# Layer 2's second products in seven instead of eight for six of eight feature groups, with paired wide operations

## The chip, the core and the metric

One NeuronCore of a Trainium2 chip runs the whole program. The metric is device time in microseconds, from the program's start to its end; the times shown are the median of several executions. The engines are TensorE (PE; its weight loads have a row of their own, PEld), VectorE (DVE), ScalarE (ACT), GpSimd (POOL) and SyncE (SP), which issues most of the DMA transfers.

## What is computed

Attention over 256 channels and two feed-forward layers, all in float32, on 6016 tokens:

```python
qn = q / (norm(q, axis=1) + 1e-06); kn = k / (norm(k, axis=1) + 1e-06)
s = kn.transpose(0, 2, 1) @ qn / tau          # 256 x 256
a = exp(s - s.max(-1)); a /= a.sum(-1) + 1e-09
x = (v @ a).reshape(6016, 256)
h = x @ w_in                                  # 256 -> 2048
x = (h * clip(h + 3, 0, 6) / 6) @ w_out       # layer 1, 2048 -> 256
h = maximum(x @ w_in2, 0)                     # 256 -> 2048
out = (h * h) @ w_out2                        # layer 2, 2048 -> 256
```

## The kernel before

**Precision.** A float32 operand is split into a high part (a copy to a 32-bit matmul format, on ACT) and a low part (the operand less its high part, on DVE). One product of a 128x128 weight block and n columns is three matmuls: high by high, low by high, high by low.

**Tiling.** The tokens go in six *pairs* of two column blocks of n columns: n is 512 in five pairs and 448 in the last. The 2048 features go in eight *groups* of 256, two row blocks of 128. So a group's first products form a 2x2 by 2x2 block product, and so do its second products. The main loop walks over layer, pair and group; each iteration records its operations.

**Seven products for eight.** A 2x2 block product takes eight products, or seven in Strassen's manner (Winograd's variant) with sums of operands beforehand and sums of results behind. First products are done in seven almost everywhere; the sums of the tokens' blocks are t1 to t4, made in `tokens`. Second products of layer 2 are done in seven for the groups in `S2SET`: of pairs 1 to 4 the groups 0, 2, 4, 6, of pair 5 the groups 0, 2, 4. Their operands are three of the squared blocks themselves (`items_direct`: d2, d3, d1) and four sums t1 to t4 (`items_sums`: t5 takes t1, t7 takes t3, t6 takes t2, t4 takes t4). The other groups do eight (`items_plain`).

**A group of layer 2 from pair 1 on** (`first7s`). Seven first products p1, p2, p6, p7, p5, p4, p3 go into two PSUM banks X and Y by turns. ACT copies X or Y out (`snap`, L1589), DVE adds the next result (`total`, L1595) into one of four result blocks R0 to R3, and ReLU and square follow: on ACT (L1602, L1608) for three of them, on DVE (L1615) for one. A bank is taken again by the next product, which therefore waits for that copy or that sum. Then each block is split (`split`, L1623 on ACT, L1627 on DVE). For a group by seven, `tail` makes t1 by a DVE sum (L1680) and t3, t2, t4 by three transfers that POOL issues and that add a block to another in SBUF (`move`, L1637), each waiting for the one before. The second products of a group run among the first products of the next; its four sums run one group later still:

```python
t, d = us.get(k - 3), us[k - 1]
t7, t6, t4, t5 = items_sums(t) if t and t["seven"] else [None] * 4
...
gaps = [[t7], [], [d2], [], [d3], [d1], [t6, t5, t4]]
```

`gaps[i]` are the second products that stand behind the i-th first product on PE.

**Tokens.** While a pair runs, the next pair's tokens come from DRAM in four parts, one per group (L758); DVE makes t3 first (L780), which needs the last part. All seven operands are split (ACT L803, DVE L806) into a ring of `XS` = 9 tiles. The sums t1 to t3 have a three-block tile.

**What sets the order.** Every operation is recorded with an engine, a cost, a latency and what it depends on. PE and SP keep the order of recording. For DVE, ACT and POOL the planner (`Plan.issue`) plays the program once with these costs and takes among the ready operations the one with the earliest due time (`late`), so each engine gets one fixed order. At run time each engine takes its instructions in that order and waits at the first that is not ready.

Of the kernel before, what the change touches and what calls it, by code (L numbers as in the profile page):

```python
# [27 lines left out]
class Plan:  # L28
# [8 lines left out]
    URGENT = 6.0  # L37

# [14 lines left out]
    @staticmethod  # L53
    def pick(t, ready):

        for o in sorted(ready, key=lambda o: (max(t, o.can), o.late, o.n)):
            start = max(t, o.can)
            if not any(
                x.late < o.late - Plan.URGENT and start < x.can < start + o.cost for x in ready
            ):  # L60
                return start, min(
                    (x for x in ready if x.can <= start), key=lambda x: (x.late, x.n)
                )
        raise AssertionError

    def issue(self):
        def flat(d):
            if isinstance(d, Op):
                return [d]
            return [x for y in d or () for x in flat(y)]  # L70

        ops = self.ops
        for o in ops:
            o.deps = flat(o.deps)
        users = {id(o): [] for o in ops}
        now = 0.0
        for o in ops:
            for d in o.deps:
                users[id(d)].append(o)
            o.late = float("inf")  # L80
            if o.eng == "PE":
                o.late = now
                now += o.cost
        queue = float("inf")
        for o in reversed(ops):
            for u in users[id(o)]:
                o.late = min(o.late, u.late - o.lat - o.cost)
            if o.eng == "DMA":

                o.late = queue = min(o.late, queue - o.cost)  # L90
# [4 lines left out]
        for n, o in enumerate(ops):  # L95
            o.n, o.left, o.can = n, len(o.deps), 0.0
            if o.eng in in_order:
                in_order[o.eng].append(o)
            elif not o.left:
                ready[o.eng].append(o)  # L100
        order = []
        while len(order) < len(ops):
# [15 lines left out]
            o.start = start  # L118
# [11 lines left out]
        for o in order:  # L130
            o.fn()
# [6 lines left out]
def dve_us(n):  # L138
    return 0.07 + 0.00104 * n
# [24 lines left out]
def tile_kernel(  # L164
# [50 lines left out]
    XS, GB, WB = 9, 4, 2  # L215
# [530 lines left out]
    def tokens(l, pr, parts=False):  # L746
# [28 lines left out]
        def tt(i):  # L775
            return t["t"][:, i, :n]

        def f_t3():
            t["t"] = xr_p.tile([P, 3, TB], F32, tag="t", name=f"xt{l}{pr}")
            V.tensor_tensor(tt(2), b(1, 1), b(0, 1), ALU.subtract)  # L780

        if plain(l, pr):
            todo = [(f"b{i + 1}{j + 1}", lambda i=i, j=j: b(i, j), load) for j in range(2) for i in range(2)]
            ts = []
        else:
            c = dve_us(n)
            sub = ALU.subtract
            t3 = ordered("xt", add("DVE", c, f_t3, load, xt_r.take()))
            t1 = add("DVE", c, lambda: V.tensor_tensor(tt(0), b(0, 1), b(0, 0), sub), t3)
            t2 = add("DVE", c, lambda: V.tensor_tensor(tt(1), b(1, 1), tt(0), sub), t1)  # L790
            t4 = add("DVE", c, lambda: V.tensor_tensor(b(0, 1), b(1, 0), tt(1), sub), t2)
            ts = [t1, t2, t3, t4]
            todo = [
                ("b11", lambda: b(0, 0), load), ("b21", lambda: b(1, 0), load), ("t3", lambda: tt(2), t3),
                ("t2", lambda: tt(1), t2), ("t4", lambda: b(0, 1), t4), ("t1", lambda: tt(0), t1),
                ("b22", lambda: b(1, 1), load),
            ]
        for name, src, ready in todo:
            p = {}

            def f_hi(p=p, name=name, src=src):
# [3 lines left out]
            def f_lo(p=p, src=src):  # L805
# [5 lines left out]
            if ts:  # L811
                xt_r.reader(hi, lo)
            x_op[l, pr, name], x_done[l, pr, name], x_held[l, pr, name] = p, (hi, lo), x_r.last
        xr_r.reader(*ts)
# [619 lines left out]
    S2SET = {pr: (0, 2, 4, 6) if pr < NP - 1 else (0, 2, 4) for pr in range(1, NP)}  # L1434
    S2ALL = sorted({g for gs in S2SET.values() for g in gs})

# [3 lines left out]
    class Cell:  # L1440
        def __init__(self, make, deps=()):
            self.make, self.held, self.at = make, list(deps), None
# [70 lines left out]
    def extra_cells():  # L1513
# [3 lines left out]
        deps = all_of(stage_r)  # L1517
        for k in range(2, 4):
            cells["x", k] = Cell(lambda: stage_p.tile([P, 2, 4, P], F32R, tag="stage", name="w2x"), deps)
        cells["st"] = Cell(lambda: stage_p.tile([P, 2, 512], F32, tag="stage", name="rs"), deps)  # L1520

    def more_cells():
        deps = all_of(cv_r)
# [4 lines left out]
        st = cells["st"]  # L1528
        s0, s1 = (Cell(part_of(st, k), st.held) for k in range(2))
        deps = all_of(rt_r)  # L1530
        rt = [Cell(lambda: pools["r"].tile([P, 2, TB], F32, tag="r", name="rp"), deps) for _ in range(2)]
        rp = [Cell(part_of(x, k), deps) for x in rt for k in range(2)]
        cells["R", True] = [[e[0], e[1], m[0], m[1]], [e[2], m[2], s0, s1]]
        cells["R", False] = [rp]
        deps = all_of(wA_r)
        g4 = [Cell(lambda: wA.tile([P, 2, TB], F32R, tag="wA", name="gs"), deps) for _ in range(4)]
        deps = all_of(g_r)
        for _ in range(4):
            x = Cell(lambda: pools["g"].tile([P, 2, 2, TB], F32R, tag="g", name="gs"))
            g4.extend(Cell(part_of(x, k), deps) for k in range(2))  # L1540
        names = ["d3", "d2", "d1", "t1", "t3", "t2", "t4", "p0", "p2", "p3", "p1", "d0"]
        cells.update(zip(names, g4))
        deps = all_of(h_r)
        cells["f5"] = [Cell(lambda: h_p.tile([P, TB], F32, tag="h", name="f5"), deps) for _ in range(2)]
        deps = all_of(hp_r)
        hp = [Cell(lambda: pools["hp"].tile([P, 2, TB], F32, tag="hp", name="hs")) for _ in range(2)]
        q = [Cell(part_of(x, k), deps) for x in hp for k in range(2)]
        cells["fz"], cells["s1"] = q[:2], q[2]
        cells["X"], cells["Y"] = (Cell(lambda: psum("A", "xy"), [A_r.take()]) for _ in range(2))

    def bank_cells(k):
# [3 lines left out]
        )[4 * k - 4 : 4 * k]:  # L1555
            cells[name] = Cell(lambda tag=tag: psum(tag, tag), all_of(ring))

    def first7s(pr, g):
# [4 lines left out]
        even = g % 2 == 0  # L1563
        sets = cells["R", even]
        R = sets[g // 2 % len(sets)]
        names = ("d0", "d1", "d2", "d3") if even else ("p0", "p1", "p2", "p3")
# [32 lines left out]
        def relu(k, src, *deps):  # L1599
            return add(  # L1600
                "ACT", act_us(n) + 0.08,
                lambda: A.activation(R[k].ap()[:, :n], src.ap()[:, :n], AF.Relu), *deps,  # L1602
            )

        def square(k, *deps):
            def f():
                r = R[k].ap()[:, :n]
                A.activation(r, r, AF.Square)  # L1608

            return add("ACT", act_us(n), f, *deps)  # L1610

# [7 lines left out]
        def split(k, cell, *deps):  # L1619
            c = cells[cell]  # L1620

            def f_hi():
                A.activation(c.ap()[:, 0, :n], R[k].ap()[:, :n], AF.Copy)  # L1623
# [434 lines left out]
```

## Time and profile before

| | |
|---|---|
| median of 3 runs | 1030.91 us (1029.73 to 1032.05) |
| the profiled execution | 1029.68 us, its span 1027.9 us |
| PE busy | 1020.8 us, 99% of the span, 4565 matmuls recorded |
| PE weight loads | 854.9 us, 83% |
| DVE, ACT busy | 866.5 us (84%), 795.3 us (77%) |
| POOL busy | 69.4 us (7%) |
| DMA | 174.10 MB; hardware queue 45.3%, software queue 8.3% of 16 engines' span |

Attention takes the first 50 us or so, layer 1 and the first pair of layer 2 run to about 626 us, and pairs 1 to 5 of layer 2 fill the rest; a pair takes about 79 us and a group a little under 10. Busy time of an engine is the union of its instructions' times. Matmuls overlap at their ends, so two matmuls that start 0.34 us apart still show as busy all the time between them; the starts tell more than the busy share.

### The profile page before, as it was taken

What the parts mean: (1) busy time and instruction counts of PE and PEld (TensorE: products, weight loads), DVE (VectorE), ACT (ScalarE), POOL (GpSimd) and SP (SyncE); (2) the same over time, 40 slices, a digit from 0 to 9 for tenths busy, and PEclk for the clock granted to TensorE, in tenths of its full rate; (3) what the DMA queues carried; (4) which work ended last, traced back from release to release, by engine and by line L of the source; (5) the groups of instructions that cost most, each with busy time, mean ns of one, the idle gap of its engine ahead of it and who ended that gap; (6) DMA issues with size and microseconds to landing.
All of it is one profiled execution on the core that took longest, in us unless ns stands there. A gap on an engine that the chain in (4) does not pass through costs nothing.

```text
span 1027.9 us, 13018 instructions
## 1 busy us (share of the span) xinstructions
PE 1020.8 (99%) x4565; PEld 854.9 (83%) x4565; DVE 866.5 (84%) x1372; ACT 795.3 (77%) x1287; POOL 69.4 (7%) x78
## 2 busy tenths in 40 slices
PE   9999999999999999999999999999999999999998
PEld 8888888888888888888998888788888878888897
DVE  4999988888989898898878977689888878888876
ACT  6787667677777777677768878889889879789785
POOL 3400000000000000000000000111111111111110
PEclk9999999999999999999999999999999999999999
DMA  9658347344544544635744424755665565565661
GB/s 363 262 178 249 125 152 230 135 146 177 172 161 160 193 169 150 230 106 197 266 152 171 149 72 135 204 134 141 180 162 149 156 176 133 169 176 123 169 160 45
DMA packets 62609, 174.10 MB, mean 169 GB/s; under 512 B 6992, under 2 KB 10192, under 8 KB 61264
## 3 DMA queue, kind: packets, MB, share of 16 engines
q1 hardware_dynamic: 54336, 158.62, 45.3%
q0 software_dynamic: 8208, 14.65, 8.3%
q8 instruction: 36, 0.59, 0.2%
q14 instruction: 29, 0.24, 0.1%
HBM read 126.35 MB, written 32.24 MB: 154 GB/s over the span
## 4 chain that ended last, share of the span: by engine, by line
PE 95%; DVE 2%; ACT 1%; DMA 1%; issue 0%; SPq 0%; DVEq 0%
PE acc L1361 10%; PE acc L1362 10%; PE acc L1367 10%; PE xy L1577 6%; PE xy L1579 6%; PE xy L1578 6%; PE A L1268 4%; PE A L1269 4%; PE A L1270 4%; PE s L900 4%; PE acc L1713 3%; PE acc L1715 3%; PE acc L1714 3%; PE B L1268 2%; PE B L1270 2%; PE B L1269 2%
## 5 line engine op out<-in xcount | busy, mean ns | idle before, releaser
L1362 PE MATMUL acc<-g,wo 128*128 128x512 f32 (+1 forms) x448 | 173.0, 386 | 0.0
L1361 PE MATMUL acc<-g,wo 128*128 128x512 f32 (+1 forms) x448 | 173.0, 386 | 0.0
L1154 DVE TENSOR_TENSOR g<-r,g 128x1024 fp32r<-128x1024 f32 (+1 forms) x112 | 135.0, 1205 | 24.0 <-ACT g L1150 23.8
L1150 ACT ACTIVATE g<-r 128x1024 fp32r<-128x1024 f32 (+1 forms) x112 | 117.1, 1046 | 46.4 <-DVE r L1124 45.7
L1367 PE MATMUL acc<-g,wo 128*128 128x512 f32 (+1 forms) x448 | 136.5, 386 | 0.0
L1637 POOL DMA_DIRECT2D rs<-rs x57 | 49.2, 862 | 915.8 <-ACT rp L1589 607.5
L1627 DVE TENSOR_TENSOR gs<-rs,gs 128x512 fp32r<-128x512 f32 (+1 forms) x137 | 90.0, 673 | 18.3 <-ACT gs L1623 16.7
L1367 PEld LDWEIGHTS acc<-g,wo 128*128 128x128 f32 x448 | 84.2, 188 | 16.0
L1361 PEld LDWEIGHTS acc<-g,wo 128*128 128x128 f32 x448 | 84.2, 188 | 15.9
L1362 PEld LDWEIGHTS acc<-g,wo 128*128 128x128 f32 x448 | 84.1, 188 | 15.9
L1623 ACT ACTIVATE gs<-rs 128x512 fp32r<-128x512 f32 (+1 forms) x137 | 80.1, 614 | 7.9 <-DVE rs L1615 7.6
L1119 ACT ACTIVATE r<-hp,three 128x1024 f32<-128x1024 f32 (+1 forms) x40 | 45.3, 1131 | 48.9 <-DVE hp L1301 48.8
L1293 ACT ACTIVATE hp<-A 128x512 f32<-128x512 f32 (+1 forms) x96 | 56.5, 589 | 9.2 <-PE A L1270 8.2
L1577 PE MATMUL xy<-xt,w 128*128 128x512 f32 (+1 forms) x160 | 63.1, 395 | 0.1
L1579 PE MATMUL xy<-xt,w 128*128 128x512 f32 (+1 forms) x160 | 61.7, 386 | 0.0
L1578 PE MATMUL xy<-xt,w 128*128 128x512 f32 (+1 forms) x160 | 61.7, 386 | 0.0
L1124 DVE SCALAR_TENSOR_TENSOR r<-r,hp 128x1024 f32<-128x1024 f32 (+1 forms) x40 | 47.9, 1197 | 15.8 <-ACT r L1119 15.4
L1627 DVE TENSOR_TENSOR gs<-rp,gs 128x512 fp32r<-128x512 f32 (+1 forms) x80 | 52.3, 670 | 5.6 <-ACT gs L1623 5.6
L1595 DVE TENSOR_TENSOR rp<-xy,rp 128x512 f32<-128x512 f32 (+1 forms) x60 | 40.4, 674 | 17.3 <-ACT rp L1589 14.2
L1713 PE MATMUL acc<-gs,wo 128*128 128x512 f32 (+1 forms) x141 | 54.3, 385 | 0.2 <-DVE c L1827 0.2
L1715 PE MATMUL acc<-gs,wo 128*128 128x512 f32 (+1 forms) x141 | 54.3, 385 | 0.0
L1714 PE MATMUL acc<-gs,wo 128*128 128x512 f32 (+1 forms) x141 | 54.3, 385 | 0.0
(376 smaller groups left out, 2617.3 us busy)
## 6 DMA issues: line engine op xcount, KB each, us to landing
w<-w1d SPq DMA_DIRECT2D x176, 448.0 KB, 4.3
rs<-rs POOLq DMA_DIRECT2D x48, 256.0 KB, 3.3
qk<-in_qk_dram SPq DMA_DIRECT2D x8, 1024.0 KB, 15.0
w1d<-wA SPq DMA_DIRECT2D x16, 448.0 KB, 5.6
xr<-in_vT_dram SPq DMA_DIRECT2D x5, 1024.0 KB, 6.8
x2d<-o SPq DMA_DIRECT2D x20, 256.0 KB, 3.8
w1d<-wA SPq DMA_DIRECT2D x16, 256.0 KB, 2.6
w1d<-w SPq DMA_DIRECT2D x14, 256.0 KB, 3.0
```

What stands on the lines that cost most here:

```text
L1150: A.activation(t["g"][:, a:b, 0, :n], t["t"][:, a:b, :n], AF.Copy)
L1154: V.tensor_tensor(g[:, a:b, 1, :n], t["t"][:, a:b, :n], g[:, a:b, 0, :n].bitcast(F32), ALU.subtract)
L1361: T_.matmul(acc[b, e][:, :n], w(e, 0), gh_, start=first_of, stop=False)
L1362: T_.matmul(acc[b, e][:, :n], w(e, 1), gh_, start=False, stop=False)
L1367: T_.matmul(acc[b, e][:, :n], w(e, 0), gl_, start=False, stop=last_of_b)
L1577: T_.matmul(ps, wh, xh, start=start, stop=False, skip_group_check=True)
L1578: T_.matmul(ps, wl, xh, start=False, stop=False, skip_group_check=True)
L1579: T_.matmul(ps, wh, xl, start=False, stop=True, skip_group_check=True)
L1627: V.tensor_tensor(x[:, 1, :n], R[k].ap()[:, :n], x[:, 0, :n].bitcast(F32), ALU.subtract)
L1713: T_.matmul(ps, wh, gh, start=first, stop=False, skip_group_check=True)
L1714: T_.matmul(ps, wl, gh, start=False, stop=False, skip_group_check=True)
L1715: T_.matmul(ps, wh, gl, start=False, stop=last, skip_group_check=True)
```

## The change

Six groups of eight do their second products in seven: 0, 1, 3, 4, 5, 6 of pairs 1 to 4 and 0, 1, 3, 4, 5 of pair 5. So 29 groups instead of 19.

The result blocks now stand in two tiles of two blocks each (`Duo`): A2 holds R0 and R1, B2 holds R2 and R3. There are three such sets, on the spaces `stage`, `r` and `hp` (`RSET`); the remaining groups (2 and 7, of pair 5 groups 2 and 6) use single blocks. With a set, ReLU and square of R2 and R3, and their split, are one operation of 2n columns each; R0's ReLU and square go to DVE instead of R3's. Of the four sums, t3 and t2 are made by one transfer of twice the width that adds R2, read twice, to R0 and R1, and t4 by a second transfer; their splits are one wide and one single. The four sums' products no longer run two groups behind a group but at the places in `S2AT`, three to four groups behind; t1's product joins the direct ones.

`tokens` makes t1, t2 and t4 in place of the token blocks, so the third tile shrinks to one block and the ring of operand tiles grows to 10. Six instead of four sets of weight sums are made (`sums2`), in the first pair of layer 2.

The planner plays the program 200 times; after each time `blame` lowers the rank of the operations on which PE waited, and the order of the shortest play is kept.

```diff
+    ROUNDS = 200
...
+    def blame(self):
+        for o in self.ops:
+            if o.eng != "PE" or o.idle < 0.03:
+                continue
+            x = o
+            while x.deps:
+                x = max(x.deps, key=lambda d: d.start + d.cost + d.lat)
+                if x.eng in ("PE", "DMA") or o.start - x.start > 12.0:
+                    break
+                x.rank -= 0.5 * min(1.0, o.idle + 0.2)
...
+        for _ in range(self.ROUNDS):
+            end, order = self.run()
+            if best is None or end < best[0]:
+                best = end, order
+            self.blame()
...
-    XS, GB, WB = 9, 4, 2
+    XS, GB, WB = 10, 4, 2
...
+        t3 = ordered("xt", add("DVE", dve_us(n), f_t3, load, xt_r.take()))
+        t1 = less((0, 1), (0, 1), (0, 0), t3)
+        b11 = split_x("b11", lambda: b(0, 0), load)
+        b21 = split_x("b21", lambda: b(1, 0), load)
+        t2 = less((0, 0), (1, 1), (0, 1), t1, b11)
+        t4 = less((1, 0), (1, 0), (0, 0), t2, b21)
...
-    S2SET = {pr: (0, 2, 4, 6) if pr < NP - 1 else (0, 2, 4) for pr in range(1, NP)}
+    S2SET = {pr: (0, 1, 3, 4, 5, 6) if pr < NP - 1 else (0, 1, 3, 4, 5) for pr in range(1, NP)}
+    S2AT = {0: 4, 1: 5, 3: 6, 4: 7, 5: 9, 6: 10}
+    LAST_AT = {(NP - 1, 5): 8}
...
+        rs = [Duo(lambda: stage_p.tile([P, 2, TB], F32, tag="stage", name="rs"), deps) for _ in range(2)]
...
+            h, lo = ((x[:, :, k, :n] if size > 1 else x[:, k, :n]) for k in range(2))
+            V.tensor_tensor(lo, src.ap()[..., :n], h.bitcast(F32), ALU.subtract)
...
-                nc.gpsimd.dma_start(R[k].ap()[:, :n], R[j].ap()[:, :n], accum_op=ALU.add)
+                s = src.ap()[:, :n]
+                if size > 1:
+                    s = s.unsqueeze(1).to_broadcast([P, size, n])
+                nc.gpsimd.dma_start(dst.ap()[..., :n], s, accum_op=ALU.add)
...
+            if B2:
+                r = act(AF.Relu, 0.08, B2, B2, 2, h22, h21)
+                done[2] = done[3] = act(AF.Square, 0, B2, B2, 2, r)
...
+        def chain():
...
+            x = split(R[1], part("t14", 0), 1, t1)
+            u["t1"] = (part("t14", 0), *x)
+            done["t32"] = move(A2, R[2], 2, x, done[2])
+            done["t4"] = move(R[3], R[1], 1, done["t32"], u[3][1:])
+        def split_t():
+            x = split(A2, cells["t32"], 2, done["t32"])
+            u["t3"], u["t2"] = (part("t32", 0), *x), (part("t32", 1), *x)
+            c = part("t14", 1)
+            u["t4"] = (c, *split(R[3], c, 1, done["t4"]))
...
-                    gaps = [[t7], [], [d2], [], [d3], [d1], [t6, t5, t4]]
+            if d and d["seven"]:
+                d["chain"]()
+                d2, d3, d1, t5 = items_direct(d)
+                for i, x in zip((4, 5, 6, 6), (d2, d3, d1, t5)):
+                    gaps[i].append(x)
+            elif d:
+                x = items_plain(d)
+                for i, j in zip((0, 2, 4, 5, 6, 6, 6, 6), (0, 4, 1, 3, 6, 2, 7, 5)):
+                    gaps[i].append(x[j])
+            if t:
+                t7, t6, t4 = items_t(t)
+                gaps[0].append(t7)
+                gaps[2].append(t6)
+                gaps[6].insert(-1, t4)
...
+            us[k]["splits"]()
+            if k + 1 in due:
+                us[due[k + 1]]["split_t"]()
```

**Order on PE.** The middle of one group of pair 3 (xy: the banks X and Y; xt1 to xt3: the tokens' sums; acc01, acc11: result banks of d2 and t6). Before:

```order
L1577 MATMUL xy_5584<-xt2_6795,w1_7158 128x512
L1578 MATMUL xy_5584<-xt2_6795,w1_7158 128x512
L1579 MATMUL xy_5584<-xt2_6795,w1_7158 128x512
L1713 MATMUL acc01_5681<-gs_5640,wo14_5021 128x512
L1714 MATMUL acc01_5681<-gs_5640,wo14_5021 128x512
L1715 MATMUL acc01_5681<-gs_5640,wo14_5021 128x512
L1577 MATMUL xy_5600<-xt3_6785,w1_7158 128x512
L1578 MATMUL xy_5600<-xt3_6785,w1_7158 128x512
L1579 MATMUL xy_5600<-xt3_6785,w1_7158 128x512
L1577 MATMUL xy_5584<-xt1_6833,w1_7158 128x512
L1578 MATMUL xy_5584<-xt1_6833,w1_7158 128x512
L1579 MATMUL xy_5584<-xt1_6833,w1_7158 128x512
```

Now:

```order
L1620 MATMUL xy_5601<-xt2_6745,w1_7115 128x512
L1621 MATMUL xy_5601<-xt2_6745,w1_7115 128x512
L1622 MATMUL xy_5601<-xt2_6745,w1_7115 128x512
L1778 MATMUL acc11_5916<-gs_5858,w2x_5378 128x512
L1779 MATMUL acc11_5916<-gs_5858,w2x_5378 128x512
L1780 MATMUL acc11_5916<-gs_5858,w2x_5378 128x512
L1620 MATMUL xy_5614<-xt3_6766,w1_7115 128x512
L1621 MATMUL xy_5614<-xt3_6766,w1_7115 128x512
L1622 MATMUL xy_5614<-xt3_6766,w1_7115 128x512
L1620 MATMUL xy_5601<-xt1_6785,w1_7115 128x512
L1621 MATMUL xy_5601<-xt1_6785,w1_7115 128x512
L1622 MATMUL xy_5601<-xt1_6785,w1_7115 128x512
```

Between the first products on xt2 and xt3 stands now t6, of a group three to four back, and d2 of the group just before has moved behind the product on xt1.

**Order on DVE.** Pair 3, where the next pair's tokens (xr14) are first used (xt14: the tile of t3; rp, rs, hs: result blocks). Before:

```order
L1627 TENSOR_TENSOR gs_5673<-rs_5653,gs_5673 128x512
L1627 TENSOR_TENSOR gs_5768<-rs_5803,gs_5768 128x512
L1680 TENSOR_TENSOR rs_5653<-rs_5653,rs_5594 128x512
L1595 TENSOR_TENSOR rp_5668<-xy_5600,rp_5668 128x512
L780 TENSOR_TENSOR xt14_7277<-xr14_7088 128x512
L789 TENSOR_TENSOR xt14_7277<-xr14_7088 128x512
L1595 TENSOR_TENSOR rp_5686<-xy_5584,rp_5686 128x512
L1627 TENSOR_TENSOR gs_5732<-rp_5668,gs_5732 128x512
```

Now:

```order
L1638 TENSOR_TENSOR rp_5696<-xy_5614,rp_5696 128x512
L1663 TENSOR_TENSOR gs_5719<-rs_5612,gs_5719 128x512
L1645 SCALAR_TENSOR_TENSOR rp_5671<-rp_5671 128x512
L1813 TENSOR_TENSOR f5_5742<-xy_5614,f5_5742 128x512
L802 TENSOR_TENSOR xt14_7267<-xr14_6964 128x512
L812 TENSOR_TENSOR xb11_7238<-xr14_6964,xb11_7238 128x512
L1638 TENSOR_TENSOR hs_5823<-xy_5614,hs_5823 128x512
L1663 TENSOR_TENSOR gs_5679<-rp_5696,gs_5679 128x2x512
L1663 TENSOR_TENSOR gs_5719<-hs_5840,gs_5719 128x512
```

Before, t3 (L780) stood behind the first sum of group 5 (rp_5668). Now it (L802) stands behind all sums of group 5 (rp_5671, rp_5696) and its Y bank's last flush (L1813), at the first sum of group 6 (hs_5823). Both orders are alike in pairs 2 to 4.

**Order on ACT.** One group by seven (rp: its blocks; L1632 is the copy of a bank). Now:

```order
L1632 ACTIVATE rp_5671<-xy_5601 128x512
L1658 ACTIVATE gs_5698<-rs_5612 128x512
L1632 ACTIVATE rp_5696<-xy_5601 128x512
L1658 ACTIVATE gs_5858<-hs_5823 128x2x512
L1632 ACTIVATE rp_5696<-xy_5614 128x512
L1658 ACTIVATE gs_5719<-rs_5612 128x512
L1652 ACTIVATE rp_5671<-xy_5601 128x512
L1652 ACTIVATE rp_5696<-rp_5696 128x1024
L1652 ACTIVATE rp_5671<-rp_5671 128x512
L1652 ACTIVATE rp_5696<-rp_5696 128x1024
L1632 ACTIVATE rs_5746<-xy_5601 128x512
```

Before, the same stretch held single operations only. Now a wide split (gs_5858) stands ahead of the third copy, and a wide square ahead of the next group's first copy.

The built program has 4418 matmul instructions where it had 4448, all 30 fewer in layer 2. On DVE the splits' low parts and t1's sums were 217 + 19 single operations; they are 129 + 29 single and 59 wide. On ACT the ReLUs and squares from SBUF and the splits were 417 single operations; they are 209 single and 119 wide. POOL issued 57 single moves; it issues 29 single and 29 wide. Up to the first pair of layer 2 the orders differ only in the tokens' sums and in a few exchanged neighbours.

## Rows read from the trace of the kernel before

**Rows 1.** Page, part 1: busy time, share, instructions; part 2: granted clock

```profile
PE 1020.8 (99%) x4565; PEld 854.9 (83%) x4565; DVE 866.5 (84%) x1372; ACT 795.3 (77%) x1287; POOL 69.4 (7%) x78
PEclk9999999999999999999999999999999999999999
```

**Rows 2.** Stretches: us, busy (instructions) by engine, granted clock, DMA share, GB/s

```profile
300.00:400.00 100.00, 100.00 (x443) 82.86 (x442) 92.70 (x142) 76.61 (x109) 0.00 (x0) 1.00 0.45 155
578.00:617.00 39.00, 39.00 (x174) 32.31 (x173) 32.28 (x56) 30.07 (x42) 0.00 (x0) 1.00 0.24 82
697.00:776.00 79.00, 79.00 (x348) 64.88 (x347) 67.10 (x109) 67.77 (x125) 10.31 (x12) 1.00 0.60 160
776.00:855.00 79.00, 78.23 (x342) 63.50 (x341) 65.54 (x106) 66.53 (x122) 10.31 (x12) 1.00 0.59 158
855.00:934.00 79.00, 78.95 (x347) 64.44 (x346) 66.27 (x108) 67.34 (x124) 10.32 (x12) 1.00 0.58 155
```

**Rows 3.** Timeline of PE, pair 3: start us, us, instruction, [idle before <-releaser]

```profile
838.14 0.39 PE L1577 MATMUL xy<-xt,w 128*128 128x512 f32 x1
838.37 0.39 PE L1578 MATMUL xy<-xt,w 128*128 128x512 f32 x1
...
839.28 0.39 PE L1715 MATMUL acc<-gs,wo 128*128 128x512 f32 x1
840.39 0.50 PE L1577 MATMUL xy<-xb,w 128*128 128x512 f32 x1 [0.72 <-DVE rp L1595]
840.72 0.39 PE L1578 MATMUL xy<-xb,w 128*128 128x512 f32 x1
...
845.06 0.39 PE L1579 MATMUL xy<-xb,w 128*128 128x512 f32 x1
845.49 0.50 PE L1577 MATMUL xy<-xt,w 128*128 128x512 f32 x1
845.83 0.39 PE L1578 MATMUL xy<-xt,w 128*128 128x512 f32 x1
```

**Rows 4.** Timeline of PE, pair 5

```profile
1014.34 0.37 PE L1577 MATMUL xy<-xb,w 128*128 128x448 f32 x1
1014.54 0.37 PE L1578 MATMUL xy<-xb,w 128*128 128x448 f32 x1
```

**Rows 5.** Waits: engine line <- waited for: us in total, times, longest us

```profile
PEld xy L1577 <- DVE rp L1595: 4.8, 15, 1.1
```

**Rows 6.** Timelines of DVE and SP (its DMA issues), pair 3

```profile
835.24 0.68 DVE L1595 TENSOR_TENSOR rp<-xy,rp 128x512 f32<-128x512 f32 x1
838.44 0.69 DVE L780 TENSOR_TENSOR xt<-xr 128x512 f32<-128x512 f32 x1 [2.52 <-DMA xr<-x2d]
839.04 0.68 DVE L789 TENSOR_TENSOR xt<-xr 128x512 f32<-128x512 f32 x1
839.65 0.68 DVE L1595 TENSOR_TENSOR rp<-xy,rp 128x512 f32<-128x512 f32 x1
...
830.87 0.43 SPq L758 DMA_DIRECT2D xr<-x2d  x1
```

**Rows 7.** Groups of instructions, narrow and wide: busy us, mean ns of one | idle before

```profile
L1154 DVE TENSOR_TENSOR g<-r,g 128x1024 fp32r<-128x1024 f32 (+1 forms) x112 | 135.0, 1205 | 24.0 <-ACT g L1150 23.8
L1627 DVE TENSOR_TENSOR gs<-rs,gs 128x512 fp32r<-128x512 f32 (+1 forms) x137 | 90.0, 673 | 18.3 <-ACT gs L1623 16.7
L1150 ACT ACTIVATE g<-r 128x1024 fp32r<-128x1024 f32 (+1 forms) x112 | 117.1, 1046 | 46.4 <-DVE r L1124 45.7
L1623 ACT ACTIVATE gs<-rs 128x512 fp32r<-128x512 f32 (+1 forms) x137 | 80.1, 614 | 7.9 <-DVE rs L1615 7.6
L501 DVE TENSOR_TENSOR op<-op 128x128 f32<-128x128 f32 x28 | 7.0, 285 | 0.1
L1637 POOL DMA_DIRECT2D rs<-rs x57 | 49.2, 862 | 915.8 <-ACT rp L1589 607.5
```

**Rows 8.** DMA: software queue's share; issues xcount, KB each, median us to landing

```profile
q0 software_dynamic: 8208, 14.65, 8.3%
w<-w1d SPq DMA_DIRECT2D x176, 448.0 KB, 4.3
rs<-rs POOLq DMA_DIRECT2D x48, 256.0 KB, 3.3
wo<-wo2d SPq DMA_DIRECT2D x4, 512.0 KB, 5.8
DMA to landing us min/median/max: 3.4/5.3/7.5
```

More of the change, by code (lines that the diff above doesn't have):

```diff
@@ L54, in pick, with run @@
     def pick(t, ready):
-        for o in sorted(ready, key=lambda o: (max(t, o.can), o.late, o.n)):
+        for o in sorted(ready, key=lambda o: (max(t, o.can), o.rank, o.n)):
             start = max(t, o.can)
             if not any(
-                x.late < o.late - Plan.URGENT and start < x.can < start + o.cost for x in ready
+                x.rank < o.rank - Plan.URGENT and start < x.can < start + o.cost for x in ready
             ):
                 return start, min(
-                    (x for x in ready if x.can <= start), key=lambda x: (x.late, x.n)
+                    (x for x in ready if x.can <= start), key=lambda x: (x.rank, x.n)
                 )
         raise AssertionError
[L66 to L90, printed above, removed]
+    def run(self):
+        ops, users = self.ops, self.users
         in_order = {"PE": [], "DMA": []}
@@ L94, in issue @@
         at = {"PE": 0, "DMA": 0}
-        for n, o in enumerate(ops):
-            o.n, o.left, o.can = n, len(o.deps), 0.0
+        for o in ops:
+            o.left, o.can, o.idle = len(o.deps), 0.0, 0.0
             if o.eng in in_order:
@@ L117, in issue @@
             start, o = best
-            o.start = start
+            o.start, o.idle = start, start - free[o.eng]
             free[o.eng] = start + o.cost
@@ L773, in b, with split_x, f_hi, f_lo @@
             return t["r"][:, i, j * n : (j + 1) * n]
-        def tt(i):
-            return t["t"][:, i, :n]
         def f_t3():
[L779 to L798, printed above, removed]
+            t["t"] = xr_p.tile([P, TB], F32, tag="t", name=f"xt{l}{pr}")
+            V.tensor_tensor(t["t"][:, :n], b(1, 1), b(0, 1), ALU.subtract)
+        def split_x(name, src, ready):
             p = {}
-            def f_hi(p=p, name=name, src=src):
+            def f_hi():
                 p["x"] = x_p.tile([P, 2, TB], F32R, tag="x", name=f"x{name}")
                 A.activation(p["x"][:, 0, :n], src(), AF.Copy)
-            def f_lo(p=p, src=src):
+            def f_lo():
                 V.tensor_tensor(p["x"][:, 1, :n], src(), p["x"][:, 0, :n].bitcast(F32), ALU.subtract)
@@ L1562, in first7s @@
         seven = by7(l, pr, g)
[L1563 to L1566, printed above, removed]
+        A2, B2 = cells["R"][RSET[pr, g]] if (pr, g) in RSET else (None, None)
+        R = A2.part + B2.part if A2 else cells["R4"]
         X, Y = cells["X"], cells["Y"]
@@ L1650, in steps @@
             Y.use(h11)
-            g0 = square(0, relu(0, R[0], h11))
-            if not seven:
-                u[0] = split(0, names[0], g0)
+            done[0] = both(0, h11)
             yield
@@ L1662, in steps @@
             h22 = total(3, X, p5, sn7)
-            g3 = both(3, h22)
-            u[3] = split(3, names[3], g3)
+            if not B2:
+                done[3] = act(AF.Square, 0, R[3], R[3], 1, act(AF.Relu, 0.08, R[3], R[3], 1, h22))
             yield
@@ L1693, in steps, with part, splits @@
-            if seven:
-                u["tail"] = tail
-            yield
+            done[1] = act(AF.Square, 0, R[1], R[1], 1, r)
+            yield
+        def part(name, k):
+            return cells[name].part[k]
+        def splits():
+            if B2:
+                x = split(B2, cells["d23"], 2, done[2])
+                u[2], u[3] = (part("d23", 0), *x), (part("d23", 1), *x)
+            else:
+                for k in (2, 3):
+                    c = part("d23", k - 2)
+                    u[k] = (c, *split(R[k], c, 1, done[k]))
+            if seven:
+                c = cells["d1"]
+                u[1] = (c, *split(R[1], c, 1, done[1]))
+            else:
+                for k in (0, 1):
+                    c = part("p01", k)
+                    u[k] = (c, *split(R[k], c, 1, done[k]))
@@ L2002, in tile_kernel @@
     x = items_plain(us[max(us)])
+    t7, t6, t4 = items_t(us[due[max(us) + 1]])
+    t7()
+    t6()
     x[0]()
```

249 lines of the change are left out of this document (141 added, 108 removed).

## The prediction

> **What bounds the kernel now.** I read the page's busy shares first, then the stretches of layer 2, then the starts of the matmuls. PE is busy for 1020.8 of the span's 1027.9 us at full granted clock (2.4 GHz); DVE and ACT stand at 84% and 77% [rows 1]. That makes PE the suspect, but busy time can hide gaps. So look at starts: in pair 3 two matmuls of 512 columns start 0.23 us apart (838.14, 838.37) [rows 3], which at 79 us a pair gives room for 348; the stretch from 697 has 348, that from 776 has 342 [rows 2]. Pairs of layer 2 thus run back to back but for a handful of waits. The waits view has them in one row: weight loads of first products waited 15 times for DVE's sum, 4.8 us in all, longest 1.1 [rows 5]. PE's work is the bound; the waits are worth at most some 5 us more. Beside it DVE works 66.3 us of a 79 us pair and ACT 67.3 (the stretch from 855) [rows 2].
>
> A rule speaks against this reading. By the Trainium skill, "Trainium Kernel Development and Optimization", Performance Expectations, matmul busy time is a bad metric because matmuls are pipelined, and the weight loads' busy share is a good one; here that is 83%, which would leave PE a sixth of the time free. The trace settles it by the spacing of starts: layer 1, back to back with 443 matmuls in 100 us, also shows 82.9% weight loads, and the layer 2 pair from 697 shows 64.88 of 79, or 82.1% [rows 2]. 83% is what a full PE looks like here.
>
> **The change part by part.**
>
> *Products removed.* Ten more groups do seven second products for eight: two more in each of pairs 1 to 4, two in pair 5. A product is three matmuls. That is 24 matmuls of 512 columns and 6 of 448, and the built program indeed has 30 fewer. Spacing is 79 us over 348, 0.227 us, for 512 columns [rows 2], and some 0.203 for 448 (1014.34 to 1014.54) [rows 4]. 24 x 0.227 + 6 x 0.203 = 5.45 + 1.22 = **6.7 us** off the path, since PE is the path.
>
> *The late tokens.* In pair 3 DVE met t3 before its last DMA part had landed: the part was issued at 830.87, t3 started at 838.44 after 2.52 us of idleness, and the sum that PE needed stood behind it and began at 839.65 [rows 6]. PE's starts are 839.28, then 840.39 and 840.72, then 845.06, 845.49 and 845.83: against 0.227 each that lost 0.88 + 0.10 + 0.20 + 0.11 = 1.3 us [rows 3]. The new order puts t3 behind all the sums of group 5, at the start of group 6, where before it stood behind the first sum of group 5; that is nine products of three matmuls, some 6 us, later, and the landing that was 2.5 us late, of at most 7.5 us [rows 8], is then early. I take **1.3 us** gained. Bounds: nothing, to all 4.8 us of the waits [rows 5].
>
> *DVE and ACT.* Here the change pays. A narrow DVE operation takes 0.614 us of its time (66.27 us for 108 [rows 2]); a wide one 0.532 more, by the means 1205 and 673 ns [rows 7], so 1.146. Over five pairs 78 fewer narrow and 59 more wide ones: 67.6 - 47.9 = 19.7 us, or 3.9 a pair. DVE then has 70.2 us of work in 79 - 6 x 0.227 = 77.6 us, 90%. On ACT 208 fewer narrow (67.34 us for 124, 0.543 each) and 119 more wide (0.543 + 1.046 - 0.614 = 0.975 [rows 7]): 116.0 - 112.9 = 3 us, 0.6 a pair; ACT then has 67.9 of 77.6, 88%. Neither is the bound by work. Layer 1 has run PE without a gap beside a DVE at 92.7 of 100 us (from 300) [rows 2]. So the price on the path is nothing, as long as the order keeps the wide ones away from what PE waits for. What hides it is slack: in a group PE has two products, 1.36 us, between the one that fills a bank and the one that takes it again or adds to it, and the copy or sum takes 0.6 to 0.7. The order on PE keeps this distance. What a copy can lose behind a wide operation is 1.046 - 0.614 = 0.43 us [rows 7], within the slack of 0.6 once, not twice. The wide squares make a group's d2 and d3 ready later, and these were moved two products (1.36 us) later. I take **0**, with a bound of 4.7 us: one short wait in each of 39 groups, at 0.12 us, which is what the first matmul after a wait takes longer (840.39 to 840.72) [rows 3]. Below zero is not excluded either; that is the other 3.5 us of the waits.
>
> *Moves.* 58 issues for 57, half of them wide. POOL has 862 ns each and nothing else to do [rows 7]. A move of 256 KB lands in 3.3 us; for 512 KB the row of a plain transfer of that size gives 5.8, twice 3.3 gives 6.6 [rows 8]. Two in a row are then done some 12 us after their start, and the products that use them run three to four groups (28 us or more) later, where they used to run within one group. Cost 0; were the cover gone, PE would wait the landing, 3 to 7 us once per group. The traffic grows by half: the software queue's 8.3% of 1028 us is 85 us of transfer time, 22% of the 390 us of pairs 1 to 5, and becomes 33%; the DMA share there goes from 0.59 [rows 2] to about 0.7. The weights of a group (4.3 us to landing [rows 8]) have most of a group's 9.5 us. Cost 0, bound: another wait for tokens of 1.3 us a pair, 5 us.
>
> *Smaller things.* Two more sets of weight sums are each two operations of 512 (0.67), four of 128 (0.29) and one on ACT: about 5 us of DVE in the first pair of layer 2, which has DVE at 32.3 of 39 us (from 578) [rows 2, 7]; hidden. Sums in place and a tenth tile change no count; the new chain (t2 waits for the split of b11, t4 for that of b21) has a whole group of cover. The 200 passes leave attention and layer 1 almost as they were, where PE has nothing to gain. The end of the program has the same last steps. Nothing for any of these.
>
> **Sum.** 6.7 + 1.3 = 8.0 us off the profiled execution: 1029.7 becomes 1021.7. That execution stands 1.2 us under the median of 1030.91; against the median, **1022.9 us**.
>
> **The rivals.** A difference under about 0.2%, 2.1 us, cannot be told from none here.
>
> *Waits eat part of it.* With DVE at 90% and ACT at 88% every delay lasts longer. If each of the 39 groups has one short wait, the 4.7 us above, and the 1.3 us is not gained: 1030.9 - 6.7 + 4.7 = 1028.9. For it: one wide split does stand ahead of the third copy on ACT. Against: before, 40 groups had only 15 such waits.
>
> *DVE becomes the bound, and it is slower.* DVE is idle 12.7 us of a pair now, and this idleness is not free choice: low parts wait for ACT's high parts, sums for products (L1627 alone idled 18.3 us) [rows 7]. If it stayed, a pair would last 70.2 + 12.7 = 82.9 us instead of 79, five pairs 19 us more: 1050. The point that decides is 8.8 us of idleness a pair; below that the pair is shorter than before. If the idleness only falls to 10.5, it is 1.7 x 5 = 8.5 us: 1039. Against it: 7.3% idle is enough for DVE in layer 1 [rows 2], wide operations mean fewer handovers, and the order has given d2, d3 and the moves more room.
>
> *PE is not the bound.* Then its fewer matmuls turn to idle time and nothing changes: 1030.9. This is how it would go by the rule on weight loads above. The spacing of starts speaks against it.
>
> *All waits go*, as a better order may do: 1030.9 - 6.7 - 4.8 = 1019.4.
>
> **How the numbers follow.** The forecast, 1020 to 1026.5: 0.62. Part eaten, 1026.5 to about 1030: 0.21, two thirds of which is still faster by over 0.2% (under 1028.8). DVE the bound: 0.09. PE not the bound: 0.04. All waits gone, under 1020: 0.04. Faster: 0.62 + 0.14 + 0.04 = 0.80. Within 0.2%: 0.07 + 0.04 = 0.11. Slower: 0.09. The range 1020 to 1029.5 leaves out 0.04 below and some 0.16 above.
>
> **What would show it.** Right: matmuls fall by 30 in number, PE's idle time stays near what it was, starts in layer 2 keep 0.227 us, pairs take about 77.5 us, the DVE wait for tokens is gone, DVE shows some 70 us a pair. Wrong: a row of PE or PEld waiting for a copy or sum with dozens of entries (the wide operations stand in the way), waits of ACT or DVE for a move's landing, or PE's busy share in layer 2 falling with DVE above 95%.

## The result and the profile after

The changed kernel takes **1040.85 us** (median of 5 runs, 1040.03 to 1041.97) against 1030.91: 1.0099 times the time before, 95% interval 1.0086 to 1.0111. It is about 10 us slower; 1022.9 was forecast. The profiled execution took 1041.97 us with a span of 1039.9. Its page, busy time, the software queue and the chain that ended last:

```profile
PE 1021.5 (98%) x4535; PEld 849.0 (82%) x4535; DVE 890.5 (86%) x1365; ACT 791.9 (76%) x1200; POOL 81.3 (8%) x79
...
q0 software_dynamic: 12064, 22.32, 12.2%
...
PE 66%; DMA 19%; issue 9%; DVE 2%; POOL 2%; ACT 1%; SPq 0%; DVEq 0%; POOLq 0%; ACTq 0%
```

PE has 30 matmuls fewer than in [rows 1], as it should, and its busy time is no shorter. The last line is the hint: a fifth of the chain is DMA. In the kernel before the same line of the page reads:

```profile
PE 95%; DVE 2%; ACT 1%; DMA 1%; issue 0%; SPq 0%; DVEq 0%
```

Which transfers these are, the DMA issues tell (KB each, median us from the start of the issue to the landing):

```profile
w<-w1d SPq DMA_DIRECT2D x176, 448.0 KB, 4.5
...
rs<-rs POOLq DMA_DIRECT2D x8, 512.0 KB, 7.1
rp<-rp POOLq DMA_DIRECT2D x8, 512.0 KB, 7.8
hs<-hs POOLq DMA_DIRECT2D x8, 512.0 KB, 8.9
```

The wide moves take 7 to 9 us where [rows 8] has 3.3 for a single one. The waits view, ACT, DVE, PE and the weight loads, has these rows (us in total, times, longest):

```profile
ACT gs L1658 <- DMA rs<-rs: 10.5, 5, 3.6
...
ACT gs L1658 <- DMA hs<-hs: 9.6, 5, 3.9
...
DVE gs L1663 <- ACT gs L1658: 22.1, 26, 3.6
...
PE xy L1778 <- DVE rp L1638: 5.0, 4, 2.9
PE xy L1778 <- ACT gs L1658: 3.0, 3, 1.6
...
PEld xy L1778 <- ACT rp L1652: 6.6, 4, 3.2
PEld xy L1778 <- ACT gs L1658: 4.3, 3, 2.0
```

The kernel before has none of them but the DVE one, whose counterpart there is as large in total, with shorter single waits:

```profile
DVE gs L1627 <- ACT gs L1623: 22.3, 22, 2.0
```

Read the rows from the top: ACT stands 20.1 us, ten times, before a split (L1658) whose move has not landed; the longest of DVE's waits for ACT's high parts come with it; PE waits at L1778, the product t5. Nine gaps of PE from pair 1 on are longer than 0.6 us, and seven of them, 9.2 us in all, stand before t5, each 2 to 3 us behind the end of such a wait of ACT. One case, pair 3, timelines of POOL, SP, ACT, DVE and PE:

```profile
804.03 1.20 POOL L1679 DMA_DIRECT2D rs<-rs  x1 [9.19 <-DVE gs L1663]
814.14 0.90 POOL L1679 DMA_DIRECT2D rs<-rs  x1 [8.91 <-DMA rs<-rs]
...
804.48 0.81 SPq L573 DMA_DIRECT2D w<-w1d  x2
805.33 0.43 SPq L783 DMA_DIRECT2D xr<-x2d  x1
...
813.87 1.06 ACT L1658 ACTIVATE gs<-rs 128x1024 fp32r<-128x1024 f32 x1 [2.66 <-DMA rs<-rs]
814.83 0.61 ACT L1652 ACTIVATE rs<-rs 128x512 f32<-128x512 f32 x1
815.35 0.61 ACT L1658 ACTIVATE gs<-rp 128x512 fp32r<-128x512 f32 x1
...
816.00 0.69 DVE L1663 TENSOR_TENSOR gs<-rp,gs 128x512 fp32r<-128x512 f32 x1 [1.93 <-ACT gs L1658]
...
814.94 0.39 PE L1780 MATMUL acc<-gs,wo 128*128 128x512 f32 x1
816.02 0.50 PE L1778 MATMUL xy<-gs,w2x 128*128 128x512 f32 x1 [0.69 <-ACT gs L1658]
816.36 0.40 PE L1779 MATMUL xy<-gs,w2x 128*128 128x512 f32 x1
```

The wide move is issued at 804.03, and SP issues the next weights half a us later and the tokens 1.3 us later. It lands at 813.84, 9.8 us after its start; the planner takes 1.3 us for the issue and 6.2 from there to the landing, 7.5. ACT, whose order is fixed, meets the split of t3 and t2 (128x1024) and stands 2.66 us. PE does not need this split for a group or more. But behind it in ACT's queue stands the split of t1 (gs<-rp, 815.35), which PE needs now. PE loses 0.85 us at t5 (814.94 to 816.02, less the spacing of 0.227).

Over the layer, by the first matmul of each group, pair 3 (a group has 14 products, 9.52 us, or 15, 10.20, in the changed kernel):

| kernel | lengths of the eight groups, us | pair |
|---|---|---|
| before | 10.20 9.57 10.22 9.62 10.20 10.69 10.54 9.67 | 80.71 |
| changed | 10.43 9.52 10.75 11.06 9.52 10.50 9.82 9.53 | 81.13 |
| changed, another landing in the planner (f1, below) | 10.24 9.52 9.52 10.24 9.52 9.52 9.72 9.55 | 77.83 |

Pair 3 is the one with the late tokens; pairs 2 and 4 of the kernel before take 79.4 and 79.7 us. From the first product of pair 1 to the last matmul it is 397.9 us before (625.80 to 1023.74), 406.2 in the changed kernel, 389.9 in f1. So 6.7 us of products went, and some 15 us of waiting came.

### The profile page after: what moved, and what is told of

Its sections match the earlier page's. It is cut to its first block, busy times and chain, and to the rows that moved or that the text cites. A ratio compares the mean times of both kernels' runs of the same rounds, so it can differ in the third digit from the quotient of the medians.

```text
span 1039.9 us, 12954 instructions
## 1 busy us (share of the span) xinstructions
PE 1021.5 (98%) x4535; PEld 849.0 (82%) x4535; DVE 890.5 (86%) x1365; ACT 791.9 (76%) x1200; POOL 81.3 (8%) x79
## 4 chain that ended last, share of the span: by engine, by line
PE 66%; DMA 19%; issue 9%; DVE 2%; POOL 2%; ACT 1%; SPq 0%; DVEq 0%; POOLq 0%; ACTq 0%
PE acc L1394 10%; PE acc L1393 10%; PE acc L1399 10%; DMA hs<-hs 7%; DMA rs<-rs 5%; PE A L1300 4%; PE A L1301 4%; DMA rp<-rp 4%; PE A L1302 4%; DMA qk<-in_qk_dram 3%; PE B L1302 2%; PE B L1301 2%; PE B L1300 2%; PE xy L1620 2%; PE xy L1622 2%
## 5 line engine op out<-in xcount | busy, mean ns | idle before, releaser
L1679 POOL DMA_DIRECT2D rs<-rs x20 | 21.4, 1069 | 712.9 <-DVE gs L1663 648.2
L1658 ACT ACTIVATE gs<-rs 128x512 fp32r<-128x512 f32 (+2 forms) x90 | 63.2, 707 | 13.1 <-DMA rs<-rs 10.5
L1663 DVE TENSOR_TENSOR gs<-rs,gs 128x512 fp32r<-128x512 f32 (+2 forms) x90 | 70.4, 788 | 3.0 <-ACT gs L1658 2.8
L1652 ACT ACTIVATE rs<-rs 128x512 f32<-128x512 f32 (+3 forms) x80 | 54.9, 716 | 3.5 <-DVE rs L1638 3.2
L1663 DVE TENSOR_TENSOR gs<-hs,gs 128x512 fp32r<-128x512 f32 (+3 forms) x48 | 42.1, 883 | 11.4 <-ACT gs L1658 11.4
L1663 DVE TENSOR_TENSOR gs<-rp,gs 128x512 fp32r<-128x512 f32 (+3 forms) x50 | 43.6, 881 | 8.1 <-ACT gs L1658 7.9
L1778 PE MATMUL acc<-gs,wo 128*128 128x512 f32 (+1 forms) x131 | 50.4, 385 | 0.0
L1780 PE MATMUL acc<-gs,wo 128*128 128x512 f32 (+1 forms) x131 | 50.4, 385 | 0.0
```

What stands on the lines that cost most here:

```text
L1658: A.activation(x[:, :, 0, :n] if size > 1 else x[:, 0, :n], src.ap()[..., :n], AF.Copy)
L1663: V.tensor_tensor(lo, src.ap()[..., :n], h.bitcast(F32), ALU.subtract)
```

## The experiments

Three theories. **A**: the planner reckons the wide moves' landing too early, and in-order ACT pays for it with whatever is queued behind. **B**: DVE and ACT, 90% and 88% full, are too full for wide operations. **C**: the transfers themselves are too slow for the kernel, by their size or the load on the queues. Ratios are to the kernel before, with 95% intervals.

**The planner's landing time, wide moves (e1, f3).**

```diff
-o = add("POOL", MOVE_US + 0.4 * (size - 1), f, *deps, lat=MOVE_LAT)
+o = add("POOL", MOVE_US + 0.4 * (size - 1), f, *deps, lat=MOVE_LAT + 5.0 * (size - 1))
```

e1 as shown; f3 has 1.0 for 5.0.

> The changed kernel, but the planner is told that a wide move lands 11.2 us after its issue (it was told 6.2; the trace of the changed kernel shows 7 to 9 at the median). Theory A (late landing): the planner put ACT's split of a move's result at a landing that comes 2 to 4 us later on the chip, and ACT's queue, in order, holds the t1 split behind it. Then ACT's waits for moves (10, 20 us in the changed kernel) fall to a few, and the time to 1023 to 1033 us. Theory B (DVE and ACT too full, 90% and 88%, so that wide operations delay short ones): nothing changes, 1038 to 1043. Theory C (the transfers themselves are too slow, by their size and by the load on the queues): landings are as late, PE then waits at t3, t2 or t4 in place of t5; 1036 or more.

> The changed kernel, the planner told 7.2 us for a wide move (6.2 before), the passes as they were. Theory A with a landing of 7.6 us behind the issue at the median: most of the lost time comes back, 1020 to 1028, but the latest landings (up to 10.7 us) still hold ACT. Theory B: 1038 to 1043. Theory C: 1036 or more.

e1: 1033.92 us, 1.0034 (1.0020 to 1.0048). ACT's waits for moves fell from 20.1 to 3.9 us and 7 us of time came back, a little less than A had. The rest sits elsewhere. One of the waits in its place, in pair 2:

```profile
ACT hs L1632 <- DVE gs L1663: 0.9, 1, 0.9
PEld xy L1620 <- ACT hs L1632: 0.9, 1, 0.9
```

A copy into a tile of results (hs, L1632) waits for the last reader of its former content, the low part of t4. That the planner, told of 11.2 us, holds the tiles longer than the chip needs is argued from its own reckoning and not shown apart. f3: **1025.99 us**, 0.9962 (0.9951 to 0.9974). One us more in one number takes 15 us off; B, which had 1038 or more in both runs, and C, which had 1036 or more, fall. Each of these runs has a new order, though, so part of a single difference can be the order's own; g1 and g2 below keep the order.

**Landing and look back (f1, f4).** The passes raise the rank of what delayed PE, but stop 12 us back, which is less than a late move and a split behind it. f1 has both lines, f4 the second alone:

```diff
...
-lat=MOVE_LAT)
+lat=MOVE_LAT + 2.0 * (size - 1))
...
-if x.eng in ("PE", "DMA") or o.start - x.start > 12.0:
+if x.eng in ("PE", "DMA") or o.start - x.start > 30.0:
```

> The changed kernel with two numbers of the planner changed: a wide move lands 8.2 us after its issue (6.2 before), and the passes look for what delayed a product up to 30 us back (12 before, which a chain of a late move and a split behind it exceeds). Same operations. With 11.2 us in the first experiment the waits for moves had shrunk from 20 to 4 us, but the planner itself left PE 16 us idle in layer 2, because it held every wide move for the full 11.2 us before its tile of sums could be used again; here its own reckoning leaves 1 us. Theory A: 1017 to 1025, faster than the kernel before. Theory B (DVE and ACT too full): 1033 or more, since the plan is as tight on both engines as that of the changed kernel. Theory C (transfers too slow for the kernel): 1030 or more, with waits of PE at t3, t2 or t4.

> The changed kernel with the passes looking 30 us back, the landing of a wide move left at 6.2 us. It parts the two edits of the fast version. Theory A: the number that matters is the landing time; the waits of ACT for moves stay at 10 us or more in all and the time at 1032 to 1041. If the longer look back is what matters, 1022 to 1027.

f1: **1023.71 us** (1022.06 to 1026.31), 0.9936 (0.9920 to 0.9953): the same operations as the changed kernel, 17 us less, and faster than both kernels. One pair of it (stretch: us, busy by engine, clock, DMA share), beside the changed kernel's:

```profile
782.50:860.40 77.90, 77.90 (x344) 63.92 (x344) 70.70 (x106) 66.81 (x108) 11.87 (x13) 1.00 0.76 183
```

```profile
786.40:867.50 81.10, 79.29 (x343) 63.49 (x342) 70.86 (x104) 66.44 (x107) 12.50 (x13) 1.00 0.73 174
```

PE without a gap beside a DVE with 70.70 us of work in 77.9, or 91%. B is out. The waits of ACT for moves in f1:

```profile
ACT gs L1658 <- DMA rs<-rs: 2.0, 2, 1.6
...
ACT gs L1658 <- DMA rp<-rp: 0.4, 1, 0.4
```

f4: 1035.47 us, 1.0046 (1.0030 to 1.0063), ACT waiting 16.5 us for moves. The landing time is the number that matters; the longer look back takes off some 5 us by itself.

**The same order, less to move (g1, g2).** Here nothing in the order changes. In both, part of t3 and t2 is left out.

```diff
 # g1: half of the columns
-s = src.ap()[:, :n]
+m = n if size == 1 else n // 2
+s = src.ap()[:, :m]
...
 # g2: t3 only
...
+d = d[:, 0, :n] if size > 1 else d[:, :n]
+nc.gpsimd.dma_start(d, s, accum_op=ALU.add)
```

> The changed kernel, order and everything else untouched, but the wide move adds only the first half of the columns of both halves of the pair (256 KB in 256 rows of 1 KB, where it is 512 KB in 256 rows of 2 KB). The other half of the columns of t3 and t2 is not computed. Theory A: the landing comes as early as the planner takes it, if bytes set it (3 to 5 us, then the time is 1017 to 1025); if the number of rows sets it the landing stays at 6 to 9 us and so does the time, 1036 to 1042. Theory B: the same work on DVE and ACT in the same order, so 1038 to 1043 whatever the landing.

> The changed kernel, order untouched, but the wide move adds to one half of the pair only (256 KB in 128 rows of 2 KB, the form of the kernel before). t2 is not computed. Theory A: landing at 3.3 to 5 us, waits of ACT for moves gone, 1017 to 1025. Theory B: 1038 to 1043.

g2: **1022.24 us**, 0.9923 (0.9907 to 0.9940). No wait of ACT for a move is left, and none of its 29 moves of t3 took more than 6.5 us from its start. g1: 1027.19, 0.9972 (0.9956 to 0.9987), ACT waiting 6.6 us: half the bytes in as many rows landed 5.3 us after the issue at the median, between the two cases, and so did the time. With the order of the changed kernel and landings within what it was planned for, its 30 fewer products show. (In g2 the t4 move is freed of its wait for the wide one too, as t2 is not written.)

**The fault put into the kernel before (e4).**

```diff
-MOVE_US, MOVE_LAT = 0.9, 6.2
+MOVE_US, MOVE_LAT = 0.9, 1.5
```

> The kernel before, its planner told that a move lands 1.5 us after its issue (it was told 6.2; its trace shows 3.3 at the median). No operation changes. Theory A: the same mistake is now in the kernel before, by about 2 us on every move; ACT shows waits for moves that it did not have, and the time rises by 3 to 20 us over 1030.9. Theories B and C: ACT has slack enough and the transfers are as fast as ever, so the time stays within 2 us of 1030.9.

1128.06 us, 1.0944 (1.0920 to 1.0968): the direction A gave, and five times its size. Waits of ACT and of PE in it:

```profile
ACT gs L1623 <- DMA rs<-rs: 84.7, 31, 7.5
...
PE xy L1577 <- ACT rp L1589: 36.2, 9, 5.9
PE xy L1577 <- DVE rp L1595: 24.2, 8, 3.7
```

Its moves land as fast as ever (3.3 us at the median). A kernel with neither wide moves nor a fuller DVE has the same illness once its planner is told a wrong landing. A's size was too small: ACT's waits alone are 84.7 us here, they pass through copies and sums to PE, and the PE clock falls as well (mean granted clock 0.962).

**Two singles for the wide move (e2, e2b, e2c).**

```diff
-done["t32"] = move(A2, R[2], 2, x, done[2])
+t3 = move(R[0], R[2], 1, x, done[2])
+t2 = move(R[1], R[2], 1, x, done[2])
...
```

e2 gave t2 the dependence on t3 as well; e2b has not; e2c is e2b with the longer look back.

> The changed kernel with the wide move of 512 KB made as two moves of 256 KB, one behind the other, into the same tile. All traffic and all wide splits stay; POOL issues some 30 more moves. Theory A: the two land 3.5 to 5.5 us after their issues, within the 6.2 the planner takes, so ACT's waits for moves shrink to under 8 us in all and the time falls to 1024 to 1034. Theory B: DVE and ACT have the same work, 1038 to 1043. Theory C: same bytes, so the landings of the pair are as late as the wide one, 1036 to 1043.

> The changed kernel with the wide move made as two moves of 256 KB, as tried before, but without the dependence of the second on the first that was put in there by the edit: the planner then held the second for the landing of the first (6.2 us), which the chip did not do (it issued them 0.5 us apart), and that plan left PE 25 us idle by its own reckoning. Here its reckoning leaves 3 us. Landings of single moves were 5.4 us after the start of the issue at the median, 11 at most, where the planner reckons 7.1. Theory A: 1019 to 1028, as the landing is now mostly within what the planner takes. Theory C (bytes and queues): the second single lands as late as the wide one did (8.3 us), 1033 to 1041.

> The same with the passes looking 30 us back, the counterpart of the fast version with two singles in place of the wide move. Theory A: 1017 to 1025, within 3 us of the fast version. Theory C: 1030 or more.

e2: 1043.27 us, 1.0128 (1.0111 to 1.0146), with no ACT wait for a move in layer 2: the added dependence made the plan itself slow, so its time decides nothing between A and C. e2b: 1032.04, 1.0019 (1.0008 to 1.0030), ACT waiting 8.7 us. e2c: 1027.16, 0.9972 (0.9959 to 0.9984). Both missed A's range from above. Two singles land late as well: of e2b's 72 moves of 512 columns, the 39 with a group's weights issued within a us of them took 6.3 us at the median behind their issue (up to 9.2), the other 33 took 3.2. This half of C holds: it is not the wide form. But f1, with the wide move and an honest number, is 3.5 us faster than e2c.

**What makes the landing late (k1).** POOL does twelve small additions into an unused tile ahead of each wide move:

```diff
...
+for _ in range(12):
+    nc.gpsimd.tensor_tensor(idle, d, d, ALU.add)
 nc.gpsimd.dma_start(dst.ap()[..., :n], s, accum_op=ALU.add)
```

> The changed kernel, but POOL does twelve small additions into a tile that nobody reads ahead of each wide move, so that the move is issued some 4 us later, behind the group's weights instead of with them; the planner knows nothing of it. In the changed kernel 25 of 29 wide moves have a group's weights issued within a us of them and land 7.3 us after their issue at the median; the 4 that have none land after 3.7 to 4.0. If the weights beside it are the cause, most of the wide moves here land 3.7 to 5.5 us after their issue. If the size or the wide form is the cause, 6 to 9 as before. The time tells little: the landing is as late as before or later, 1038 to 1060.

First the DMA view of the issues between 803 and 806 in the changed kernel, then between 820 and 825 in k1 (KB each, us to landing, the issue of 1.2 us included):

```profile
w<-w1d SPq DMA_DIRECT2D x2, 448.0 KB, 6.1
rs<-rs POOLq DMA_DIRECT2D x1, 512.0 KB, 9.8
xr<-x2d SPq DMA_DIRECT2D x1, 256.0 KB, 8.7
```

```profile
hs<-hs POOLq DMA_DIRECT2D x1, 512.0 KB, 5.0
```

With no weights beside it the move lands 3.8 us after its issue. In the changed kernel 20 of the 29 wide moves have a group's weights issued within a us of them, before or behind, and land 7.7 us after their issue at the median (5.8 to 9.5); the other nine take 3.7 to 5.4. Twelve of the 20 have no load of tokens in flight with them and still take 5.8 to 8.4. (The expectation's 25 and 4 count weights from 3 us ahead to 2 us behind, not within a us.) In k1 only three of the 29 have them within a us, and take 6.9 to 8.2; of the other 26, 24 land in 3.5 to 4.7, and two that follow the weights by 1.5 us in 6.4 and 7.4. So the landing goes with what is issued beside the move: size and form of the move are the same in both runs. The time, 1101.9 us in one run, was far above the 1060 I gave at most: the move starts later than planned, and ACT waits 69 us. Like e4 it says how dear a late landing is.

**The passes (e3, h1, h2).** e3: the changed kernel with ROUNDS = 1. h2: f1 with ROUNDS = 1. h1: the kernel before with the changed planner.

> The changed kernel with the schedule made in one pass in place of 200. It tells what the passes are worth. If the passes pack ACT and DVE so tightly to the modelled landings that a late landing hurts more (a variant of theory A), one pass is faster than the changed kernel, 1030 to 1039. If the passes do what they are for on the chip too, one pass is slower, 1042 to 1055, with more waits of PE for copies and sums. If neither, within 2 us of 1040.9.

> The kernel before with the changed planner (200 passes) and nothing else. What the passes alone are worth where the landings of moves (3.3 us) lie within what the planner is told (6.2). In the kernel before, the waits of weight loads for sums were 4.8 us; the passes can gain these at most: 1026 to 1031. If passes make a plan that is more fragile on the chip in any case, 1032 or more.

> The kernel with 8.2 us for wide moves, made in one pass in place of 200. If the passes carry a large part, as between the changed kernel and its one-pass form (12 us), 1031 to 1037; if the right landing time is all that was wanted, 1023 to 1026.

e3: 1053.26 us, 1.0226 (1.0201 to 1.0251), so the passes are worth 12 us there, as its second case had it. h2: 1037.73, 1.0073 (1.0052 to 1.0093), 14 us over f1 and just above the 1037 of its first case. h1: **1027.44**, 0.9966 (0.9953 to 0.9980): 2.9 us from the passes alone. The right landing and the passes are both wanted, and of f1's gain over the kernel before the passes alone give about half: against h1 it is some 3 us (0.9936 and 0.9966 of the same kernel). Not tried was a planner that keeps wide moves and weights apart in time; this one knows nothing of what else the DMA engines carry.

## Why the prediction was wrong

*Products removed, 6.7 us*: right in number (4535 for 4565), and in f1 the starts keep their 0.227 us. f1's stretch of layer 2 is 8.0 us shorter than before (389.9 for 397.9), which is the sum forecast, but partly by luck: the passes, priced at nothing, alone make that stretch 3.0 us shorter (394.9 in h1), so beside h1 the change leaves 5.0 of it.

*The late tokens, 1.3 us*: right in what was to go. DVE has no wait for xr<-x2d in layer 2 any more, where [rows 6] had 2.52 us, though the tokens land later (7.7 us at the median, [rows 8] 5.3). How much time that gave is not shown: no run parts it from the passes.

*DVE and ACT, 0*: right. Forecast 70.2 and 67.9 us of work a pair; f1 has 70.70 and 66.81 beside a PE without a gap.

*Moves, "Cost 0"*: **the step that failed**, in two places. First the landing. "A move of 256 KB lands in 3.3 us; for 512 KB ... 5.8 ..., twice 3.3 gives 6.6" took a row whose moves mostly stood apart from the weights: only 2 of the 57 in the kernel before had a group's weights issued within a us of them, and these two took 5.0 and 6.2 us behind their issue, the others 2.45 at the median. In the changed kernel 20 of 29 wide moves have them, because the weights are issued as the seventh first product of a group ends, and in these 20 the low part that releases the move comes at about the same time; they land 7.7 us after their issue at the median and 9.5 at most. The rise of the DMA share was forecast (to about 0.7; 0.73 came), but what it does to a landing was priced at nothing. By the Trainium skill, "DMA: Bandwidth & Descriptors", Anatomy of one DMA, a transfer takes about 2.0 us and its bytes at 436 GB/s: an estimate of 3.2 us for 512 KB. The nine moves without weights within a us of them take 0.5 to 2.2 us more than that; for the 7.7 us of the others that fit has no term.

Second, who waits. "The products that use them run three to four groups later" looks for the first reader on PE. The first waiter was an instruction that nobody needed soon, ACT's split, put by the planner at the landing it believed in; what stood behind it was needed at once. The 28 us of cover belonged to the split's result, not to its place in the queue. The bound of 5 us that the prediction set here was far passed: 17 us lie between the changed kernel and f1.

*Smaller things, the 200 passes at nothing*: wrong by 2.9 us in the kernel before (h1) and by 12 to 14 in the changed one. I had looked at attention and layer 1, where nothing moves, and not at the pairs. "The end of the program has the same last steps" was wrong by 0.9 us: the four last output transfers are issued later against the last matmul, and from its start to the end it is 5.0 us (5.4 in f1) where it was 4.2. And the 0.12 us for a short wait is 0.10 by the row that it names, which makes the 4.7 a 4.0.

*The rivals*: "DVE becomes the bound" had the time that came, 1039, for another reason. Its mark, PE starved with DVE above 95%, did not show: DVE is at 87% of pair 3. "PE is not the bound", the rule on weight loads, falls with f1 and g2: fewer matmuls did shorten the kernel. What the prediction named as a sign of error, "waits of ACT or DVE for a move's landing", is what came; it had no price there.

## What to carry to other kernels

A transfer's duration is that of the company it keeps: read it from issues that start beside the same other transfers as the new one will, and look at what releases both. In an engine with a fixed order ask of each wait what is queued behind it; the distance to the first user of its own result is no cover for these. In a planner an estimate that is too short by about a us can cost more than one that is too long by several: told of 6.2 us this kernel takes 1040.85, of 11.2 (e1) 1033.92, of 7.2 (f3) 1025.99. And a search that packs the order to its model wants a model that is right.

## What the runs showed of the hardware

**PE's clock after a gap.** Two gaps of the changed kernel, of 1.8 and 3.0 us, were followed by a stretch at the lower of PE's two levels, 1.2 GHz. Timeline of PE, then the granted clock (column before the DMA share) of a stretch behind the first gap, of the one from 934 behind the second, and of the one after it:

```profile
929.14 0.39 PE L1780 MATMUL acc<-gs,wo 128*128 128x512 f32 x1
932.38 0.47 PE L1778 MATMUL xy<-gs,w2x 128*128 128x512 f32 x1 [2.85 <-DVE rp L1638]
...
934.06 0.63 PE L1778 MATMUL C<-gs,w2x 128*128 128x512 f32 x1
934.48 0.63 PE L1779 MATMUL C<-gs,w2x 128*128 128x512 f32 x1
934.91 0.63 PE L1780 MATMUL C<-gs,w2x 128*128 128x512 f32 x1
```

```profile
900.00:903.00 3.00, 3.00 (x8) 2.17 (x7) 2.39 (x5) 2.97 (x7) 0.22 (x1) 0.50 1.03 183
...
934.00:938.00 4.00, 4.00 (x12) 3.15 (x11) 2.28 (x5) 2.96 (x5) 0.33 (x1) 0.60 0.76 131
938.00:948.00 10.00, 10.00 (x45) 8.27 (x45) 9.60 (x15) 9.18 (x15) 2.10 (x2) 1.00 0.54 136
```

PE was at work again for over a us when the spacing went from 0.227 to 0.427 us, for eight matmuls. That is 8 x 0.20 = 1.6 us on top of the 3.0, about 3 us in all for the two gaps. The other seven gaps over 0.6 us, up to 1.0, had no such sequel. In e4, with gaps of several us in every pair, the clock's mean is 0.962.

**Landings.** In the changed kernel a 256 KB move with a group's two weight transfers issued within a us of it lands 5.9 us after its issue at the median, the others 2.5; a 512 KB one 7.7, the others 4.1. The Trainium skill, "SBUF — State Buffer", SBUF: two separate sides, has a rule by which a DMA issued by GpSimd looks blocked while DVE runs an operation that takes the port pair the two share. The traces speak against it as the cause here: in k1 the move started at 848.60 landed 3.8 us after its issue with DVE busy all that time, and in the changed kernel the one at 918.67 took 9.4 us with DVE busy for 54% of them.
